# A linear-attention recurrence fused with a squared-ReLU layer: r in a four-token layout, a smaller copy of w, v cast on GpSimd's queue, and a searched order

## Chip, cores and metric

The kernel runs on one core of one Trainium2 chip. Its metric is the device time of an execution in microseconds; lower is better. Engines: PE is TensorE, ACT ScalarE, DVE VectorE, POOL GpSimd, and SP SyncE, which here only issues DMAs.

## The reference

Four batches, eight heads, 768 tokens, 48 features a head (`B, H, S, D = 4, 8, 768, 48`). An attention with a decaying state goes first:

```python
for t in range(S):
    cur = einsum('bhd,bhe->bhde', u * k[t], v[t])
    y[t] = einsum('bhd,bhde->bhe', r[t], state + cur)
    state = w[:, None] * state + einsum('bhd,bhe->bhde', k[t], v[t])
```

Then the heads are joined to `x` of 3072 x 384, and the layer is `relu(x @ w_in)**2 @ w_out` with `w_in` 384 x 2048 and `w_out` 2048 x 384. Inputs and outputs are float32.

## The kernel before

**Tiling.** The tokens go in chunks of 128. A unit is one chunk of one batch, so there are 24, in the order chunk by chunk (`units`, four batches a chunk). Within a chunk the recurrence is done by matmuls: r is multiplied by a power of w that grows with the token's place in its chunk, k by one that falls (`scale`, line 321, into the bf16 tile `rkw`). Heads go in pairs, padded from 48 to 64 features.

**One unit.** r, k and v are loaded by SP (`load`, line 300), each 128 tokens x 8 heads x 48 in rows of 192 bytes. `scale` is two DVE instructions. `rkw` is then turned so that features lie on partitions (`rkT`): for units 0 to 5 (`NPE = 6`) by PE (`turn`, line 341) and an ACT eviction (line 345), for the others by a DMA transpose on SP's queue (`turn_dma`, line 330). `at` (line 358) makes the 128 x 128 products of k and r, `mask` (line 370) keeps their upper triangle, `sums` (lines 378 and 383) makes the diagonal term with u and the unit's contribution to the state, `diag_v` (line 392), `state_add`, `state_decay` and `state_cast` (lines 400 to 412) carry on the state, `y_mm` (lines 421 and 427) and `evict_y` (line 436) make y. v is cast to bf16 by ACT (`cast_v`, line 325). y is turned by PE and ACT for units 0 to 5 (lines 452 and 456), otherwise by a DMA transpose (line 445).

**The layer.** `mm1` (line 468) makes blocks of 128 x 512 of the hidden layer, each followed by a ReLU on ACT (line 476) and a square on ACT or DVE (lines 483 and 485; `SQUARES = 'AMAMAAAM'` gives the engine of each in turn, A for ACT). `mm2` (line 492) multiplies by `w_out`, ACT evicts (line 499), SP stores (line 528). Some units go through `mm1` in pairs (`GROUPS`). The last unit is done in two column parts (`mm2_half`, line 508).

**Weights.** `w_in` and `w_out` are loaded in four quarters each, as a casting DMA by POOL (`weights`, lines 306 to 312). Before each, POOL copies one column of an r, k or v tile into `gate`, so the transfer is not issued before that tile has landed. `FRONT` lists the quarters with their gate tiles: w_in's first is gated on k of unit 1, all others on k of unit 3.

**Order.** The order on every engine is written by the class `Plan`, not found at run time. Each step has an engine, a cost in us, what it needs, what buffers and PSUM banks it takes, and a rank; for a DMA, `move` has the costs of its transfer. `Plan.run` plays the engines forward in time and always gives a free engine the ready step of lowest rank. Up to a planned time of 16 us, PE gets fill matmuls on a constant tile (`fill`, line 276) where it has nothing ready. Each engine then runs its list in order and waits on semaphores.

**Powers of w.** `wrow` is w as one row of 384, copied to all 128 partitions (line 222); `lnw` is its logarithm (line 241); `wpos` and `wneg` are exponentials with a scale for each partition (line 245). `rkw_b` are `NPAD = 5` padded buffers whose padding DVE clears (line 252).

Of the kernel before, what the change touches and what calls it, by code (L numbers as in the profile page):

```python
# [16 lines left out]
class Plan:  # L17
# [9 lines left out]
    def __init__(self, lags, cold, spare):  # L27
        self.lags = lags
        self.cold = cold
        self.spare = spare  # L30
        self.steps = []
        self.at = {}
        self.users = {}
        self.place = {}

    def add(self, key, engine, cost, emit, needs=(), rank=0.0, new=(), uses=(), move=None):
        s = dict(key=key, engine=engine, cost=cost, emit=emit, rank=rank, new=new, move=move)
        s["needs"] = [n for n in needs if n is not None]
        self.at[key] = s
        self.steps.append(s)  # L40
        for x in tuple(new) + tuple(uses):
            self.users.setdefault(x, []).append(s)

    def run(self, room, banks, count):
# [10 lines left out]
        begin, until, tight, loose = self.spare  # L55
        held[0] = "spare"
# [7 lines left out]
        def ready(s, e):  # L64
            if s["move"]:
                return s["end"] + moved
# [36 lines left out]
        while left:  # L103
            if held[0] == "spare" and t > until:
                held[0] = None
            for e, mine in todo.items():
# [5 lines left out]
                for s in mine:  # L112
                    if s["move"] and sum(x[1] / x[0]["move"][0] * x[0]["move"][3] for x in queues[e]) > 1.5:
                        continue
                    if all(done(self.at[k], e) for k in s["needs"]) and fits(s):
                        mine.remove(s)
                        left -= 1
                        for x in s["new"]:
                            if x[0] in banks:
                                n = min((n for n in held if held[n] is None), key=lambda n: since[n])  # L120
# [42 lines left out]
def kernel(  # L163
# [33 lines left out]
    loads = ctx.enter_context(tc.tile_pool(name="loads", bufs=6))  # L197
# [5 lines left out]
    banks = [psum.tile([128, 512], F32, name=f"bank{n}") for n in range(8)]  # L203
    plan = Plan((0.9, 0.0, 0.2, 0.33, 0.12), (5.5, 1.9), (1.25, 16.0, 0.057, 0.08))

    def bank(*key):
        return banks[plan.place[key]]
# [17 lines left out]
    nc.vector.memset(warm, 1.0)  # L225
    wu = const.tile([HP, 2, 2, 64], F32)
# [3 lines left out]
    nc.gpsimd.dma_start(out=wu[:, 1, :, :D], in_=u.rearrange("(p o) d -> p o d", o=2))  # L230

    iota_i = const.tile([128, 1], mybir.dt.int32)
    nc.gpsimd.iota(iota_i, pattern=[[0, 1]], base=0, channel_multiplier=1)
# [4 lines left out]
    ident4 = const.tile([HP, HP], F32)  # L238
    make_identity(nc, ident4)
    lnw = const.tile([128, dm], F32)  # L240
    nc.scalar.activation(lnw, wrow, AF.Ln)
    wpos = const.tile([128, H, D], F32)
    wneg = const.tile([128, H, D], F32)
    for wx, by in ((wpos, up), (wneg, down)):
        nc.scalar.activation(wx.rearrange("p h d -> p (h d)"), lnw, AF.Exp, scale=by)
# [15 lines left out]
    st32 = [const.tile([128, HP, D], F32, name=f"st32_{b}") for b in range(B)]  # L261
    stb = [const.tile([128, HP, 2 * D], BF16, name=f"stb_{b}") for b in range(B)]
    for b in range(B):
        nc.vector.memset(stb[b], 0.0)

    wend_c = const.tile([128, HP], F32)
    wend = wend_c.unsqueeze(2).to_broadcast([128, HP, D])
# [27 lines left out]

    def load(i, name):
        c, b = units[i]
        src = {"rt": r, "kt": k, "vt": v}[name]
        x = loads.tile([C, H, D], F32, name=name)
        nc.sync.dma_start(  # L300
            out=x, in_=src[b, :, c * C : (c + 1) * C, :].rearrange("h s d -> s h d")
        )
# [14 lines left out]
    def scale(i, x):  # L317
        t = tiles[i]
        t["rkw"] = rkw_b[i % NPAD]
        src, wx = (t["kt"], wneg) if x else (t["rt"], wpos)  # L320
        nc.vector.tensor_tensor(t["rkw"][:, x, :, :, :D], pair(src), pair(wx), ALU.mult)  # L321

    def cast_v(i):
        tiles[i]["vb"] = work.tile([C, H, D], BF16, name="vb")
        nc.scalar.copy(tiles[i]["vb"], tiles[i]["vt"])  # L325

    def turn_dma(i):
        t = tiles[i]
        t["rkT"] = work.tile([128, 2, HP, C], BF16, name="rkT")
# [5 lines left out]
    def turn(i, x):  # L335
        t = tiles[i]
        t["tp", x] = bank("h", i, "rk", x).bitcast(BF16)[:, : HP * C].rearrange("p (a c) -> p a c", a=HP)
        if x == 0:
            t["rkT"] = work.tile([128, 2, HP, C], BF16, name="rkT")
        for p in range(HP):  # L340
            nc.tensor.transpose(t["tp", x][:, p, :], t["rkw"][:, x, p].rearrange("p o e -> p (o e)"), identb)  # L341
# [198 lines left out]

    add("w", ACT, 3.9, None, rank=-1e3)
    add("wk", ACT, 0.48, None, rank=-1e3, needs=["w"])
    copy("begin", SP, 0.74, None, rank=-1e3)
    add("wu", POOL, 4.6, None, rank=-1e3)
# [3 lines left out]
    add("wend", ACT, 0.4, end_columns, rank=10, needs=["copied"])  # L548
# [165 lines left out]
```

## Time and profile before

| | us |
|---|---|
| median of 3 runs | 178.38 (178.34 to 178.59) |
| the profiled execution | 179.7 |
| its span | 177.9 |
| PE busy, of it fill matmuls | 167.5, 11.9 |
| DVE busy | 128.7 |
| ACT busy | 128.8 |
| POOL busy | 11.4 |

The span is the time from the first to the last instruction of the profiled execution; the execution's own time has what lies around it as well. Busy time of an engine leaves out instructions that issue DMAs or handle semaphores. PE counts as busy in fill matmuls, so a high share there does not mean useful work. The granted clock of TensorE is full in all 40 slices of the span.

### The profile page before, as it was taken

Reading aid. Unit: us, or ns where it says so; the run is one execution under the profiler, and the core shown is the slowest. Engines: PE = TensorE matmul, PEld = TensorE weight load, DVE = VectorE, ACT = ScalarE, POOL = GpSimd, SP = SyncE. Lnnn points to the kernel's source line nnn. Section 1 sums busy time; section 2 is a strip of 40 time slices with the busy share of each in tenths; the row PEclk is TensorE's granted clock in tenths of the full one; section 3 lists DMA queues with packets and bytes.
Section 4 is the critical chain, followed back from the end, with each engine's and each line's share of the span. In section 5 each row is a group of like instructions: output and inputs, shape, how many; then the busy total and the mean of one; then the engine's idle time right before and its main releaser. Section 6 shows DMA issues by size and latency. Waiting matters only on the chain.

```text
span 177.9 us, 5106 instructions
## 1 busy us (share of the span) xinstructions
PE 167.5 (94%) x2080; PEld 135.2 (76%) x2080; DVE 128.7 (72%) x279; ACT 128.8 (72%) x268; POOL 11.4 (6%) x35
## 2 busy tenths in 40 slices
PE   7699689999999999989979999899999999999993
PEld 7599479977786886876776796786795797878762
DVE  3389996565989899769779698589598695853100
ACT  2738889999385985597488599488597499659820
POOL 7120950000000000000000000000000000000000
PEclk9999999999999999999999999999999999999999
DMA  5999999999797888869879889999998897940212
GB/s 103 192 179 181 163 197 197 208 190 179 93 208 128 169 155 171 175 132 206 174 161 185 176 166 191 133 201 185 163 199 172 187 201 135 314 135 0 71 67 90
DMA packets 107385, 29.05 MB, mean 163 GB/s; under 512 B 101985, under 2 KB 106849, under 8 KB 107361
## 3 DMA queue, kind: packets, MB, share of 16 engines
q1 hardware_dynamic: 104976, 25.37, 75.1%
q0 software_dynamic: 2240, 3.15, 10.0%
q8 instruction: 16, 0.26, 0.6%
q10 hardware_dynamic: 144, 0.20, 0.6%
q14 instruction: 9, 0.07, 0.1%
HBM read 20.65 MB, written 4.72 MB: 143 GB/s over the span
## 4 chain that ended last, share of the span: by engine, by line
PE 57%; DMA 18%; DVE 17%; issue 3%; ACT 2%; SPq 1%; ACTq 0%
PE bank L492 22%; PE bank L468 22%; DMA rkT<-rkw 8%; DMA rt<-in_r_dram 5%; DVE am L370 4%; DVE rkw L321 4%; DVE yb L436 3%; PE bank L358 3%; DMA xT<-yb 2%; PE bank L276 2%; DMA wrow<-in_w_dram 2%; DVE dv L392 2%; DVE g L485 2%; PE bank L421 1%; PE bank L508 1%
## 5 line engine op out<-in xcount | busy, mean ns | idle before, releaser
L468 PE MATMUL bank<-xT,w_in_q 128*128 128x128 bf16 (+1 forms) x864 | 71.8, 237 | 0.5 <-ACT xT L456 0.3
L476 ACT ACTIVATE gr<-bank 128x512 f32<-128x512 f32 x96 | 55.0, 601 | 19.5 <-PE bank L468 18.9
L468 PEld LDWEIGHTS <-w_in_q 128*128 128x128 bf16 x864 | 64.4, 114 | 3.3 <-issue 0.7
L492 PE MATMUL bank<-w_out_q,g 128*128 128x384 bf16 x368 | 65.1, 326 | 0.0
L492 PEld LDWEIGHTS <-g 128*128 128x128 bf16 x368 | 34.4, 98 | 20.0
L370 DVE TENSOR_TENSOR am<-bank,smask 128x512 bf16<-128x512 f32 x48 | 31.8, 684 | 8.2 <-PE bank L358 8.1
L483 ACT ACTIVATE g<-gr 128x512 bf16<-128x512 f32 x60 | 37.3, 639 | 0.6
L485 DVE TENSOR_TENSOR g<-gr 128x512 bf16<-128x512 f32 x36 | 24.6, 687 | 13.1 <-ACT gr L476 13.0
L499 ACT COPY osb<-bank 128x384 f32<-128x384 f32 x23 | 11.0, 484 | 10.1 <-PE bank L492 7.9
L412 ACT CAST stb<-st 64x192 bf16<-64x192 f32 x40 | 14.0, 350 | 5.1 <-DVE st L406 4.4
L350 DVE TENSOR_TENSOR rk<-rkT 128x512 bf16<-128x512 bf16 x24 | 10.1, 422 | 7.7 <-DMA rkT<-rkw 5.6
L321 DVE TENSOR_TENSOR rkw<-rt,wpos 128x384 bf16<-128x384 f32 x24 | 13.2, 552 | 2.5 <-DMA rt<-in_r_dram 1.7
L436 DVE TENSOR_TENSOR yb<-bank,dv 128x384 bf16<-128x384 f32 x24 | 13.3, 555 | 2.3 <-PE bank L427 1.7
L392 DVE TENSOR_TENSOR dv<-vb,bank 128x384 f32<-128x384 bf16 x24 | 13.1, 545 | 2.6 <-PE bank L383 2.6
L321 DVE TENSOR_TENSOR rkw<-kt,wneg 128x384 bf16<-128x384 f32 x24 | 13.2, 551 | 0.6 <-DMA kt<-in_k_dram 0.3
L276 PE MATMUL bank<-warm 128*128 128x128 bf16 x108 | 11.9, 275 | 1.1 <-DVE warm L225 1.1
L358 PE MATMUL bank<-rkT 64*128 64x128 bf16 x192 | 9.8, 222 | 2.8 <-DMA rkT<-rkw 1.9
L325 ACT CAST vb<-vt 128x384 bf16<-128x384 f32 x24 | 12.2, 508 | 0.2
L402 DVE TENSOR_TENSOR st<-bank,st 64x192 f32<-64x192 f32 x32 | 11.3, 352 | 0.2
L358 PEld LDWEIGHTS <-rkT 64*128 64x128 bf16 x192 | 5.5, 96 | 7.5 <-issue 2.9
L276 PEld LDWEIGHTS <-warm 128*128 128x128 bf16 x108 | 9.6, 128 | 1.4 <-DVE warm L225 1.1
L345 ACT COPY rkT<-bank 128x512 bf16<-128x512 bf16 x12 | 6.9, 585 | 4.5 <-PE bank L341 4.5
(54 smaller groups left out, 97.8 us busy)
## 6 DMA issues: line engine op xcount, KB each, us to landing
rt<-in_r_dram SPq DMA_DIRECT2D x24, 192.0 KB, 4.2
kt<-in_k_dram SPq DMA_DIRECT2D x24, 192.0 KB, 4.0
vt<-in_v_dram SPq DMA_DIRECT2D x24, 192.0 KB, 4.4
out_dram<-osb SPq DMA_DIRECT2D x23, 192.0 KB, 2.8
w_in_q<-in_moe_w_in_dram POOLq DMA_DIRECT2D x4, 384.0 KB, 7.2
w_out_q<-in_moe_w_out_dram POOLq DMA_DIRECT2D x4, 384.0 KB, 13.1
rkT<-rkw SPq DMA_TRANSPOSE x18, 3.8
xT<-yb SPq DMA_TRANSPOSE x18, 3.0
```

The costliest lines, as they stand in the source:

```text
L276: nc.tensor.matmul(out=banks[0][:, :128], lhsT=warm, rhs=warm, start=True, stop=True)
L321: nc.vector.tensor_tensor(t["rkw"][:, x, :, :, :D], pair(src), pair(wx), ALU.mult)
L358: nc.tensor.matmul(out=t["at"][o][:, p, :], lhsT=t["rkT"][sl, 1, p, :], rhs=t["rkT"][sl, 0, p, :], start=True, stop=True,)
L370: nc.vector.tensor_tensor(am, t["at"][o], smask.unsqueeze(1).to_broadcast([C, HP, C]), ALU.mult)
L392: nc.vector.tensor_tensor(t["dv"], t["vb"], t["d"].unsqueeze(2).to_broadcast([C, H, D]), ALU.mult)
L412: nc.scalar.copy(stb[b][sl, :, o * D : (o + 1) * D], st32[b][sl])
L436: nc.vector.tensor_tensor(t["yb"], t["y"], t["dv"].rearrange("p h d -> p (h d)"), ALU.add)
L468: nc.tensor.matmul(out=t["h", s][:, a], lhsT=turned, rhs=chunks[c]["xT"][:, n, b : b + m, :], start=(n == 0), stop=(n == NK - 1),)
L476: nc.scalar.activation(t["gr", s], t["h", s], AF.Relu)
L483: nc.scalar.activation(g, x, AF.Square)
L485: nc.vector.tensor_tensor(g, x, x, ALU.mult)
L492: nc.tensor.matmul(out=t["o"], lhsT=chunks[units[i][0]]["g"][:, f, units[i][1], :], rhs=w_out_q[f // 4][:, f % 4, :], start=(f == 0), stop ...
```

## The change

1. **r of units 0 to 5** is loaded as four tokens a partition: two transfers, one for the even and one for the odd heads, in rows of 768 bytes. Partition p holds tokens 4(p // 4) to 4(p // 4) + 3 of head pair p % 4. `scale` multiplies by `wfour`, and `turn` becomes a matmul with the identity whose f32 output is written with a stride of four columns, which puts the tokens in order.
2. **w** is copied as 96 elements a partition (a head pair, by p % 4). `wfour` comes from it by four exponentials. Four f32 matmuls spread the logarithm to all pairs in PSUM, from where `wneg` and `wpos` are made. Four of the PSUM banks are used for that first and taken over later.
3. **v of units 6 to 23** is loaded by POOL's casting DMA straight to bf16 (`load_v`), into eight buffers; ACT's cast and SP's load of them go.
4. **State**: the float32 state is kept at 128 x 4 x 96 (with zero off-diagonal blocks) instead of 128 x 4 x 48, so an addition and a cast are one instruction instead of two, and a decay covers twice the columns.
5. **Order**: ranks of many steps come from a table `TURNS`; some costs of the planner, the gates in `FRONT`, the numbers of buffers and `SQUARES` are others; six of the padded buffers are cleared by POOL.

```diff
-    def __init__(self, lags, cold, spare):
+    def __init__(self, lags, cold, spare, turns):
+        self.turns = turns
...
     def add(self, key, engine, cost, emit, needs=(), rank=0.0, new=(), uses=(), move=None):
+        kind, which = (key[0], key[1] if len(key) == 2 else key[1:]) if isinstance(key, tuple) else ("", key)
+        rank = self.turns.get(kind, {}).get(which, rank)
...
-    NPAD = 5
-    SQUARES = 'AMAMAAAM'
+    NPAD = 8
+    NVB = 8
+    LATE = (0.0, 0.0, 0.0)
+    SQUARES = 'AAAMAAAM'
+    TURNS = {
...
+        "rt": {
+            0: -64.166, 1: -42.375, 12: 25.855, 16: 42.933, 17: 48.579, 18: 50.891, 2: -34.64, 20: 66.748, 22:
+            72.798, 3: -23.999, 5: -7.239, 7: 5.797, 8: 7.925
+        },
+        "kt": {
+            0: -62.034, 1: -59.051, 11: 22.767, 12: 25.913, 14: 31.199, 16: 41.23, 19: 60.057, 2: -36.564, 20:
+            63.314, 22: 67.009, 23: 62.992, 3: -23.719, 4: -15.851, 6: 5.385, 7: 6.643, 9: 9.761
+        },
+        "vt": {
+            0: -53.396, 1: -30.556, 2: -24.635
+        },
...
     FRONT = (
-        ("I", 0, ("kt", 1)), ("I", 1, ("kt", 3)), ("I", 2, ("kt", 3)), ("O", 0, ("kt", 3)),
-        ("I", 3, ("kt", 3)), ("O", 1, ("kt", 3)), ("O", 2, ("kt", 3)), ("O", 3, ("kt", 3)),
+        ("I", 0, ("rt", 1)), ("I", 1, ("rt", 2)), ("I", 2, ("rt", 3)), ("O", 0, ("kt", 3)),
+        ("O", 1, ("kt", 4)), ("O", 2, ("rt", 5)), ("O", 3, ("rt", 5)), ("I", 3, ("kt", 3)),
     )
...
-    loads = ctx.enter_context(tc.tile_pool(name="loads", bufs=6))
+    loads = ctx.enter_context(tc.tile_pool(name="loads", bufs=7))
...
-    wrow = const.tile([128, dm], F32)
-    nc.scalar.dma_start(out=wrow, in_=w.rearrange("h d -> (h d)").unsqueeze(0).to_broadcast([128, dm]))
+    wrow = const.tile([128, 2 * D], F32)
+    nc.scalar.dma_start(out=wrow, in_=w.rearrange("(a o) d -> a (o d)", o=2).unsqueeze(0).to_broadcast([32, HP, 2 * D]))
...
-    for n in range(NPAD):
-        for x in range(2):
-            nc.vector.memset(rkw_b[n][:, x, :, :, D:], 0.0)
+    for n in range(2):
+        nc.vector.memset(rkw_b[n][:, :, :, :, D:].rearrange("p x a o e -> p (x a o) e"), 0.0)
...
+    for n in range(2, NPAD):
+        nc.gpsimd.memset(rkw_b[n][:, :, :, :, D:].rearrange("p x a o e -> p (x a o) e"), 0.0)
...
+    def spread_log():
+        for a in range(HP):
+            sl = slice(a * 32, a * 32 + 32)
+            nc.tensor.matmul(out=four[:, a, : 2 * D], lhsT=ones[sl], rhs=lnw[sl], start=True, stop=True)
+
+    def power_four():
+        for l in range(4):
+            nc.scalar.activation(wfour[:, l].rearrange("p o d -> p (o d)"), lnw, AF.Exp, scale=at4[:, l : l + 1])
+
+    def power(out, by):
+        nc.scalar.activation(out.rearrange("p (a o) d -> p a (o d)", o=2), four[:, :, : 2 * D], AF.Exp, scale=by)
...
+        if name == "rt" and i < NPE:
+            src = src.rearrange("(a o) (q l) d -> o q a (l d)", o=2, l=4)
+            for o in range(2):
+                nc.sync.dma_start(out=x[:, o * 4 : o * 4 + 4, :].rearrange("p l d -> p (l d)"), in_=src[o])
+        else:
+            nc.sync.dma_start(out=x, in_=src.rearrange("h s d -> s h d"))
...
+    def load_v(i):
+        c, b = units[i]
+        tiles[i]["vb"] = work.tile([C, H, D], BF16, name="vc", bufs=NVB)
+        nc.gpsimd.dma_start(out=tiles[i]["vb"], in_=v[b, :, c * C : (c + 1) * C, :].rearrange("h s d -> s h d"))
...
+            if x == 0:
+                to = t["tp", 0].rearrange("p a (q l) -> p l q a", l=4)[:, p]
+                nc.tensor.matmul(out=to, lhsT=src, rhs=identb, start=True, stop=True)
...
-        for o in range(2):
-            sl = slice(o * 64, o * 64 + 64)
-            x = tiles[i]["s"][sl, :, o * D : (o + 1) * D]
-            if c == 0:
-                nc.vector.tensor_tensor(st32[b][sl], x, wend[sl], ALU.mult)
-            else:
-                nc.vector.tensor_tensor(st32[b][sl], x, st32[b][sl], ALU.add)
+        nc.vector.tensor_tensor(st32[b], tiles[i]["s"], st32[b] if c else wend, ALU.add if c else ALU.mult)
...
-        for o in range(2):
-            sl = slice(o * 64, o * 64 + 64)
-            nc.scalar.copy(stb[b][sl, :, o * D : (o + 1) * D], st32[b][sl])
+        nc.scalar.copy(stb[b], st32[b])
...
+            copy(("vb", i), POOL, 1.1, do(load_v, i), rank=a + 50, needs=[("kt", i - 1)], move=(1.06, 16, 1.4, 0.0, LATE[0]), new=[("vc", i)])
...
-        rt=6, kt=6, vt=6, rkw=NPAD, g=2, rkT=4, vb=4, rk=4, am=8, dv=4, yb=4, xT=3, gr=6, osb=6,
+        rt=7, kt=7, vt=7, rkw=NPAD, g=2, rkT=6, vb=6, vc=NVB, rk=4, am=8, dv=4, yb=4, xT=3, gr=6, osb=6,
```

More of the change, by code (lines that the diff above doesn't have):

```diff
@@ L225 @@
     nc.vector.memset(warm, 1.0)
+    I32 = mybir.dt.int32
+    iota_i = const.tile([128, 1], I32)
+    nc.gpsimd.iota(iota_i, pattern=[[0, 1]], base=0, channel_multiplier=1)
     wu = const.tile([HP, 2, 2, 64], F32)
@@ L328, in turn_dma @@
         t = tiles[i]
-        t["rkT"] = work.tile([128, 2, HP, C], BF16, name="rkT")
+        t["rkT"] = work.tile([128, 2, HP, C], BF16, name="rkT", bufs=6)
         nc.sync.dma_start_transpose(
@@ L539 @@
     plan.fill = fill
[L541 to L544, printed above, removed]
+    add("w0", ACT, 3.2, None, rank=-1e3)
+    add("log", PE, 0.25, spread_log, rank=-1e3, needs=["w0"], new=[("log", n) for n in range(4)])
+    add("w", ACT, 1.0, power_four, rank=-1e3, needs=["w0"])
+    add("wk", ACT, 0.48, do(power, wneg, down), rank=-999, needs=["log", "w"], uses=[("log", n) for n in range(4)])
+    add("wr", ACT, 0.48, do(power, wpos, up), rank=-998, needs=["wk"], uses=[("log", n) for n in range(4)])
+    add("wu", POOL, 5.8, None, rank=-1e3)
     add("cols", PE, 0.1, spread_columns, rank=-50, needs=["wu"], new=[("h", "cols")])
@@ L547 @@
     add("uwb", POOL, 0.75, u_columns, rank=-200, needs=["copied"])
-    add("wend", ACT, 0.4, end_columns, rank=10, needs=["copied"])
+    add("end", ACT, 0.4, end_columns, rank=0, needs=["copied"])
+    add("wend", POOL, 0.8, end_blocks, rank=1.5, needs=["end"])
     for n, (what, q, gated) in enumerate(FRONT):
@@ L551 @@
             (what, q), POOL, 1.0, do(weights, gated, q, what), rank=n,
-            move=((2.35, 98, 1.25, 0.0) if what == "I" else (2.05, 78, 1.25, 0.0)), needs=[gated], uses=[gated],
+            move=((2.35, 98, 1.9, 0.0, 0.0) if what == "I" else (2.05, 78, 1.9, 0.0, 0.0)), needs=[gated], uses=[gated],
         )
@@ L586 @@
         else:
-            copy(("rkT", i), SP, 1.24, do(turn_dma, i), rank=a - 30, needs=both, move=(1.5, 26, 0.67, 1.0), new=[("rkT", i)], uses=[("rkw", i)])
+            copy(("rkT", i), SP, 1.24, do(turn_dma, i), rank=a - 30, needs=both, move=(1.5, 26, 0.67, 1.0, LATE[1]), new=[("rkT", i)], uses=[("rkw", i)])
         add(("rk", i), DVE, 0.335, do(rk, i), rank=a + 1, needs=[("rkT", i)], new=[("rk", i)], uses=[("rkT", i)])
@@ L632 @@
         else:
-            copy(("xT", i), SP, 1.2, do(x_dma, i), rank=a - 30, needs=xneed, move=(0.6, 26, 0.67, 0.4), new=xnew, uses=[("yb", i)] + xuse)
+            copy(("xT", i), SP, 1.2, do(x_dma, i), rank=a - 30, needs=xneed, move=(0.6, 26, 0.67, 0.4, LATE[2]), new=xnew, uses=[("yb", i)] + xuse)
     begun = 0
```

176 lines of the change are left out of this document (135 added, 41 removed), and 13 rows, old and new, of the table TURNS.

## The prediction

> **What bounds the kernel now.** I read the page's head first, then a table of busy time by stage, then the fill matmuls, TensorE's idle gaps, the weight transfers, and last the rates of the DMA engines.
>
> ```profile
> PE 167.5 (94%) x2080; PEld 135.2 (76%) x2080; DVE 128.7 (72%) x279; ACT 128.8 (72%) x268; POOL 11.4 (6%) x35
> ...
> DMA  5999999999797888869879889999998897940212
> ```
>
> TensorE (PE) is the bound by its share, but the share hides two things: it counts the fill matmuls of line 276, and it averages over stages. The DMA engines are full or nearly so from 4 us to 150 us. The table by stage (length; busy us of PE, PEld, DVE, ACT, POOL; clock, DMA share, GB/s):
>
> ```profile
> 0.00:16.00 16.00, 13.48 (x166) 12.37 (x167) 9.56 (x34) 8.36 (x17) 4.74 (x21) 1.00 1.02 167
> 16.00:26.70 10.70, 8.58 (x156) 7.13 (x154) 10.51 (x24) 9.21 (x20) 6.63 (x14) 1.00 1.03 173
> 26.70:60.00 33.30, 33.30 (x480) 27.12 (x478) 25.29 (x52) 27.15 (x58) 0.00 (x0) 1.00 0.99 172
> 60.00:140.00 80.00, 77.13 (x856) 60.36 (x854) 66.28 (x140) 58.72 (x126) 0.00 (x0) 1.00 0.92 172
> 140.00:175.10 35.10, 35.00 (x435) 28.23 (x433) 16.82 (x32) 25.33 (x50) 0.00 (x0) 1.00 0.55 137
> ```
>
> From 26.7 to 175.1 PE stands idle for 2.97 us in all. So time can come only from two places: what PE does not use before 26.7, and those 2.97 us. The tail after PE's last matmul is 2.8 us and is not touched. The same table for the fill alone gives 10.79 us before 16.0 and 1.14 us from 16.0 to 26.7. Useful PE work before 26.7 is therefore 2.69 + 7.44 = 10.1 us, and 16.6 us are lost there.
>
> The gaps of PE after 60 us (start, length, ..., in brackets the idle time before and its releaser):
>
> ```profile
> 80.15 0.27 PE L421 MATMUL bank<-vb,am 128*128 128x48 bf16 x4 [0.55 <-DVE am L370]
> ...
> 89.86 0.40 PE L358 MATMUL bank<-rkT 64*128 64x128 bf16 x8 [1.02 <-DMA rkT<-rkw]
> ...
> 116.08 0.40 PE L358 MATMUL bank<-rkT 64*128 64x128 bf16 x8 [0.93 <-DMA rkT<-rkw]
> ...
> 139.29 2.13 PE L468 MATMUL bank<-xT,w_in_q 128*128 128x256 bf16 x18 [0.25 <-DMA xT<-yb]
> ```
>
> They add to 2.75 us, and 2.20 of it waits for DMA transposes. These sit on SP's queue between the loads.
>
> What holds PE back before 26.7 is the weights. GpSimd issues a quarter of w_in only when its gate tile has been read, and the second gate waits long:
>
> ```profile
> 18.04 0.46 POOL L306 COPY gate<-kt 128x1 f32<-128x1 f32 x1 [7.08 <-DMA kt<-in_k_dram]
> 18.51 0.78 POOL L309 DMA_DIRECT2D w_in_q<-in_moe_w_in_dram  x1
> ```
>
> By issue plus landing, w_in's first quarter is there at 10.17 + 6.3 = 16.5, the second at 18.51 + 6.2 = 24.7, and the rest of all weights follow 2.1 to 2.8 us apart until 38.9. PE's first block of the first layer starts at 16.84, and it is saturated once the second quarter is in.
>
> The early loads of 192 KB land 1.0 to 1.1 us apart (r, k, v of unit 0 at 5.34, 6.4, 7.5, then 8.45, 9.5, 10.6): 192-byte rows at some 185 GB/s. What longer rows do is seen in 150 to 156 us, where six stores with 1536-byte rows run almost alone from the middle on:
>
> ```profile
> GB/s 9 10 3 0 8 90 128 141 209 253 256 230 215 264 217 227 258 270 253 249 203 236 358 420 358 430 369 400 369 403 379 358 399 348 348 410 338 410 369 430
> ```
>
> So 350 to 430 GB/s for 1536-byte rows, about double.
>
> **The change, part by part.** All durations are of the profiled execution: 177.9 us of span, 179.7 us in all. The runs' median is 178.38, that is span + 0.5, and I convert so.
>
> *First loads.* The copy of w shrinks from 192 to 48 KB. It now lands at 4.37, together with r of unit 0 (5.34). It saves 144 KB, which is 0.4 us at the store's rate and 0.8 at the loads'. r of a unit becomes two transfers with 768-byte rows: between 0.5 us (store rate) and 1.03 (no gain) instead of 1.03; I take 0.65, nearer to the store, as only row length differs. k of unit 0, third in the queue, then lands 0.4 to 1.2 us earlier; I take 1.1, less some 0.3 because r takes a second issue on SP (0.45 each). Six loads of r save 6 x 0.38 = 2.3 us of full DMA engines by 40 us.
>
> *Powers of w.* Before: logarithm 0.52, two exponentials 0.61 and 0.60, done at 6.07. After: a logarithm and four exponentials over 128x96. The nearest rows are 0.20 for 128x4 and 0.5 to 0.6 for 128x384, hence about 0.3 each, 1.5 together, then the two of 384 columns read from PSUM (0.6 each, as gr). That is 1.0 us more of ScalarE (ACT), but it begins earlier and r's factor needs only the first 1.5: at about 3.4 + 1.5 = 4.9 instead of 5.56. k's factor needs 0.6 more, 5.5, against k's arrival at 6.4 now. Four f32 matmuls (0.26 each in the nearest row, L281's) stand where PE runs fill. So unit 0 starts about 0.8 us earlier.
>
> *Weights' order.* The first quarter is gated on r of unit 1 instead of k of unit 1. By the new ranks the loads go r0, k0, k1, v0, r1; 2 x 0.65 + 3 x 1.03 = 4.4 us of transfer against 5.1 for the five to k1 now, with 0.5 us of w's copy less in front: about 1.2 us sooner, landing at 15.3. The larger step is the second quarter, gated on r2 (two loads later, about 3 us beside the first quarter) instead of k3: issued at about 12 instead of 18.5, landing 2.5 us or more behind the first, at 18 to 19 instead of 24.7. The third follows at 21.
>
> *What that gives PE.* From 16.0 to 26.7 PE loses 3.26 us now; with two quarters and two or three units ready, I expect 2.5 of it filled (bounds 1 and 3.2). Before 16.0, 13.3 us are lost; unit 0 is 0.8 us earlier, the attention matmuls of unit 0 now wait behind fourteen fill matmuls (8.00 to 9.70, while their operand's eviction ended at 8.83), and the one addition of a state (0.55, as yb, instead of 2 x 0.352) brings VectorE's pace from 4.17 us a unit (yb at 13.40, 17.57, 21.75) to 4.0. I take 1.3 (0.5 to 2.5). Together 3.8. ACT caps this: 3.8 us of PE are 5.7 blocks of 0.67, each a relu (0.60) and three quarters of a square (0.64 x 0.75), 1.08 in all, so 6.2 us of ACT. ACT has 4.5 us idle from 4.4 to 16.0, 1.5 to 26.7, then none (13.09 busy of 13.3 to 40.0). Less 1.0 for the powers, plus 4 x 0.2 for the state's cast, that is 5.8, not all usable. I take 3.3 for the front (1.5 to 5.3).
>
> *The strided turn of r.* 24 matmuls write f32 columns 16 bytes apart. No row here does so. Four now take 0.22 us, 0.055 each; the bounds are no loss, and L281's 0.264 each. Twelve of them (units 0 to 2) stand beside fill, twelve on the path: 0 to 2.5 us. I take 0.4, near the first bound, as they have the same columns and type as L341. The eviction, f32 instead of bf16, goes from 0.585 to 0.60.
>
> The Trainium skill's page "PSUM — Partial Sum Buffer", section Specifications (TRN2), says PSUM has 8-byte lines and that a non-contiguous pattern slows matmuls significantly. One word a line instead of two would double these matmuls; as an estimate, the twelve on the path would add 12 x 0.055 = 0.7 us, and the sum below would be 0.3 us longer.
>
> *Units 6 to 23.* ACT loses 18 casts x 0.508 = 9.1 us and 20 x (0.70 - 0.51) = 3.8 in state casts, and gains 12 squares x 0.639 = 7.7 (60 to 72 of 96). VectorE loses 12 x 0.687 = 8.2 of squares and 20 x 0.15 = 3.0 of state additions, and gains 16 x 0.2 = 3.2 in decays over 384 columns. Both run beside PE; cover is their 28% of idle time, and the 0.55 us gap behind a mask should close. SP loses 18 issues of 0.53 to 1.7 us standing in front of transposes; GpSimd gets 18 with 1024 rows each. Its rows are 0.53 to 0.58 for 128 rows and 0.75 to 0.80 for 384, so 1.3 by the line through them, 24 us in all on an engine idle since 24.7. Casting halves the bytes written, not the rows or the bytes read. Of 2.75 us I expect 1.7 back (-1 to 2.5).
>
> *Memsets.* Six pads move to GpSimd (0.2 to 0.3 each by its rows), covered by its wait from 4.4 to 7.5; uncovered they would delay u's columns by at most 1.5 us, for unit 0 only.
>
> Sum: 3.3 + 1.7 - 0.4 = 4.6. Span 173.3, median **173.8**.
>
> **The rivals.**
> *DMA stays the bound in the middle.* 0.92 of share from 60 to 140, and the two waits on transposes are waits for transfers; v still moves, only from another queue, and with eight buffers it can run ahead of what is urgent. Then the middle gives nothing: 178.4 - 3.3 + 0.4 = 175.5. Against it: transposes stood behind v's issues. The Trainium skill's page "DMA: Bandwidth & Descriptors", section Issuing engines are not separate DMA queues, has this rule: another issuing engine saves only issue time.
> *The front gives its bound.* ACT finds the room, the middle closes: 178.4 - 5.3 - 2.3 + 0.3 = 171.1.
> *Slower: casting rows load the DMA engines more.* No cast transfer is in this trace. GpSimd's queue spent 10.0% x 16 x 177.9 / 2240 = 127 ns a packet, SP's 20 ns, though for rows some six times as long. Slack is 0.08 x 80 = 6.4 us, plus 2.3 and 0.5 saved. If a cast v takes x us more than 1.03, 18x - 9.2 is lost; slower than before from x = 0.77. At x = 1.03 (double) it is 9.3 - 4.6 = 4.7 slower: 183.1. Against it: 384 KB of weights landed every 2.1 to 2.8 us beside loads.
> *Long rows of r gain nothing* (256 columns of q and a, two issues): only order is left, about 1 us: 177.4.
>
> **How the numbers follow.** Forecast 0.55, DMA-bound middle 0.17, front's bound 0.14, slower 0.11, no gain of rows 0.03. About 0.2% (0.35 us) is what a measurement can tell from no change. Faster 0.87, same 0.02, slower 0.11. The range leaves out the slower case and the far end of the front's: 170.8 to 177.6.
>
> **What would show it.** Right: second quarter of w_in landed by 19, L468 blocks dense from 18, PE saturated by some 23; idle after that under 1.5 us; no v on SP after unit 5. Wrong: L341 for r at over 0.1 us apiece; v landing late with PE or VectorE waiting for it; rkT waits over 1 us between 60 and 140; gr on ACT late before 40.

## The result, and the profile after

| | before | after |
|---|---|---|
| median of the runs, us | 178.36 (177.07 to 178.59) | 185.53 (184.99 to 187.03) |
| profiled execution, its span | 179.7, 177.9 | 185.25, 183.3 |
| PE busy, of it fill | 167.5, 11.9 | 168.8, 9.6 |
| PE idle (span less busy) | 10.4 | 14.5 |
| DVE, ACT, POOL busy | 128.7, 128.8, 11.4 | 119.2, 123.3, 30.1 |

The kernel became slower: 1.043 times the time before (95% interval 1.035 to 1.051). The forecast was 173.8. Single executions of some of the kernels below lie 6 us and more apart; a ratio leaves out those over 1.5% above the fastest of their kernel, a median counts them all. All ratios here are to runs of the kernel before on the same chip. Four chips were used (one each for e1 to e4, e5 to e8, e9 to e12 and e13 to e18), so between these groups the ratios are the safer comparison.

The head of the page of the kernel after, and its table by stage (length; busy us of PE, PEld, DVE, ACT, POOL; clock, DMA share, GB/s):

```profile
PE 168.8 (92%) x2079; PEld 135.9 (74%) x2079; DVE 119.2 (65%) x244; ACT 123.3 (67%) x246; POOL 30.1 (16%) x62
...
DMA  4999999999999999999999999989999710041022
```

```profile
0.00:16.00 16.00, 13.78 (x191) 12.49 (x191) 11.33 (x34) 9.41 (x21) 10.35 (x34) 1.00 0.87 164
16.00:26.70 10.70, 8.50 (x147) 7.99 (x147) 4.57 (x10) 8.94 (x19) 2.67 (x6) 1.00 1.16 202
26.70:60.00 33.30, 31.23 (x406) 24.06 (x407) 23.10 (x47) 23.48 (x47) 9.26 (x13) 0.95 1.39 165
60.00:140.00 80.00, 75.95 (x868) 60.41 (x866) 65.92 (x131) 55.61 (x110) 7.87 (x9) 1.00 1.23 171
140.00:180.00 40.00, 39.21 (x472) 30.91 (x469) 13.95 (x25) 25.86 (x50) 0.00 (x0) 1.00 0.29 74
```

Three things stand in it. Before 26.7 us the change does what was forecast: PE is busy for 22.28 us, of which 9.56 are fill, so 12.7 us are useful against 10.1. From 26.7 to 60, where PE had not stood idle at all, it now loses 2.07 us and some of its clock. From 60 to 140 it loses 4.05 us where it lost 2.87. The time that packets took has gone up (share 1.39 and 1.23 against 0.99 and 0.92) while the bytes have not (165 and 171 GB/s against 172 and 172).

The gaps of PE (start, length, ..., in brackets the idle time before and its releaser):

```profile
26.88 0.61 PE L488 MATMUL bank<-identb,rkw 128*128 128x128 bf16 x4 [1.03 <-DVE rkw L459]
...
31.49 0.48 PE L532 MATMUL bank<-vb,rkw 128*128 128x96 bf16 x4 [1.56 <-ACT vb L468]
...
62.95 2.87 PE L609 MATMUL bank<-xT,w_in_q 128*128 128x128 bf16 x48 [0.90 <-DMA xT<-yb]
...
72.74 2.84 PE L609 MATMUL bank<-xT,w_in_q 128*128 128x128 bf16 x48 [1.20 <-DMA xT<-yb]
...
118.24 2.02 PE L609 MATMUL bank<-xT,w_in_q 128*128 128x256 bf16 x17 [0.56 <-DMA xT<-yb]
```

The waits on `rkT` have fallen from 1.9 to 0.8 us. In their place PE stands at the head of whole blocks of the layer (L609) and waits for `xT`, the turned y. Behind the gap of 1.56 us the clock falls; the same columns in stretches of 1 us:

```profile
31.00:32.00 1.00, 0.51 (x5) 0.42 (x5) 0.28 (x1) 1.00 (x3) 0.40 (x2) 0.54 1.01 191
32.00:33.00 1.00, 1.00 (x4) 0.44 (x3) 0.93 (x2) 1.00 (x3) 1.00 (x4) 0.50 1.08 196
33.00:34.00 1.00, 1.00 (x11) 0.96 (x9) 0.97 (x3) 0.89 (x3) 1.00 (x2) 0.50 1.04 126
34.00:35.00 1.00, 1.00 (x16) 1.00 (x15) 0.15 (x1) 0.83 (x3) 1.00 (x2) 0.76 0.99 172
```

That is 0.46 + 0.50 + 0.50 + 0.24 = 1.7 us of clock. The span is 5.4 us longer: 4.1 more idle, 2.3 less fill, and 3.6 more busy time for the same work, 1.7 of it by the clock and 1.4 by the strided turn (below). But the clock cannot be the main loss: another execution of this kernel took 185.8 us at full clock.

### The profile page after: what moved, and what is told of

Same layout as the page of the kernel before. It is cut to its first block, busy times and chain, and to the rows that moved or that the text cites. A ratio compares the mean times of both kernels' runs of the same rounds, so it can differ in the third digit from the quotient of the medians.

```text
span 183.3 us, 5067 instructions
## 1 busy us (share of the span) xinstructions
PE 168.8 (92%) x2079; PEld 135.9 (74%) x2079; DVE 119.2 (65%) x244; ACT 123.3 (67%) x246; POOL 30.1 (16%) x62
## 5 line engine op out<-in xcount | busy, mean ns | idle before, releaser
L609 PE MATMUL bank<-xT,w_in_q 128*128 128x128 bf16 (+1 forms) x864 | 71.0, 238 | 4.3 <-DMA xT<-yb 2.7
L609 PEld LDWEIGHTS <-w_in_q 128*128 128x128 bf16 x864 | 65.5, 114 | 7.3 <-issue 2.5
L633 PE MATMUL bank<-w_out_q,g 128*128 128x384 bf16 x368 | 68.0, 328 | 0.6 <-ACT g L624 0.6
L624 ACT ACTIVATE g<-gr 128x512 bf16<-128x512 f32 x72 | 44.4, 640 | 0.6
L626 DVE TENSOR_TENSOR g<-gr 128x512 bf16<-128x512 f32 x24 | 16.4, 686 | 20.2 <-ACT gr L617 20.2
L464 POOL DMA_DIRECT2D vc<-in_v_dram x18 | 15.8, 892 | 64.3 <-PE bank L568 52.1
L553 ACT CAST stb<-st 128x384 bf16<-128x384 f32 x20 | 10.4, 524 | 8.4 <-DVE st L549 8.4
L456 DVE TENSOR_TENSOR rkw<-rt,wpos 128x384 bf16<-128x384 f32 x18 | 9.7, 549 | 4.6 <-DMA rt<-in_r_dram 4.6
L541 DVE TENSOR_TENSOR dv<-vc,bank 128x384 f32<-128x384 bf16 x18 | 9.8, 545 | 3.6 <-ACT g L624 3.6
L390 PE MATMUL bank<-warm 128*128 128x128 bf16 x99 | 9.6, 255 | 1.1 <-DVE warm L328 1.1
L562 PEld LDWEIGHTS <-am 128*128 128x128 bf16 x192 | 7.8, 96 | 2.7 <-DVE am L519 1.5
L549 DVE TENSOR_TENSOR st<-st,wend 128x384 f32<-128x384 f32 x16 | 8.8, 550 | 0.0
```

The lines of the kernel that those rows point to most:

```text
L464: nc.gpsimd.dma_start(out=tiles[i]["vb"], in_=v[b, :, c * C : (c + 1) * C, :].rearrange("h s d -> s h d"))
L609: nc.tensor.matmul(out=t["h", s][:, a], lhsT=turned, rhs=chunks[c]["xT"][:, n, b : b + m, :], start=(n == 0), stop=(n == NK - 1),)
L624: nc.scalar.activation(g, x, AF.Square)
L626: nc.vector.tensor_tensor(g, x, x, ALU.mult)
L633: nc.tensor.matmul(out=t["o"], lhsT=chunks[units[i][0]]["g"][:, f, units[i][1], :], rhs=w_out_q[f // 4][:, f % 4, :], start=(f == 0), stop ...
```

## The experiments

Four suspects were set against each other: the order table `TURNS`, the weights' gates in `FRONT`, r's layout, and v on GpSimd's queue.

### Taking the table and the queue out of the change

e1 empties the table, so every step has its written rank; e2 leaves the table and puts v of units 6 to 23 back on SP with ACT's cast; e3 does both; e4 is e1 with r loaded and turned as before.

```diff
-    TURNS = { ... }                                            # e1, e3, e4
+    TURNS = {}
-        for n, name in enumerate(("rt", "kt", "vt") if i < NPE else ("rt", "kt")):   # e2, e3; ACT's cast for all units
+        for n, name in enumerate(("rt", "kt", "vt")):
...
-        if name == "rt" and i < NPE:                           # e4; scaling and turn as before, too
+        if name == "rt" and i < 0:
...
```

> The changed kernel with an empty table TURNS: every step has its default rank again, all else as changed. Order theory (the searched ranks are the loss: they let y of some units, its transposes and so the next blocks come late, and hold loads of units 3 and 4 behind weights): back by 8 to 11 us, 174 to 178, TensorE idle after 35 us under 2 us instead of 5.2. Queue theory (GpSimd's casting loads of v, eight of which go out from 33 to 40 us, slow SP's loads and transposes): the loss stays, 183 to 186.

> The changed kernel with v of units 6 to 23 loaded by SP and cast by ScalarE again, the table TURNS kept. Order theory: no help, 184 to 187, as the order of y and of the blocks is unchanged. Queue theory: the share of DMA between 35 and 60 us falls from over 1.3 to about 1, the waits for xT at 63 and 73 us go, 177 to 180.

> Default ranks and v on SP and ScalarE. Order theory: v's queue is a small item, within 1.5 us of the run with default ranks alone, in either direction. Queue theory: about 177 to 179, well below the run with default ranks alone. If both matter, below both of the others.

> Default ranks, and r of units 0 to 5 loaded in 192-byte rows and turned by plain transposes again. If the long rows are worth what was forecast (2.3 us of DMA time by 40 us, unit 0 earlier), 1 to 3 us slower than the run with default ranks alone. If the strided turn (0.10 us a matmul instead of 0.055, 24 of them) eats it, within 0.5 us.

| | median us | ratio to before |
|---|---|---|
| e1 default ranks | 180.58 | 1.011 (1.000 to 1.023) |
| e2 v on SP | 185.43 | 1.043 (1.035 to 1.052) |
| e3 both | 180.40 | 1.012 (1.001 to 1.022) |
| e4 e1, r as before | 179.53 | 1.011 (1.003 to 1.018) |

The table costs 5 us of the 7.2. Neither with the table (e2 against the change) nor without it (e3 against e1) does v's queue make a difference, and r's layout makes none in this setting either (e4 against e1). The table by stage of e2 says the same of the packets' time: with v on SP its share falls to 0.90 and 0.97, about what it was before the change, and the time of the kernel stays.

```profile
26.70:60.00 33.30, 31.59 (x415) 24.34 (x410) 23.64 (x47) 24.55 (x51) 1.36 (x4) 0.95 0.90 160
60.00:140.00 80.00, 75.22 (x861) 59.30 (x859) 60.52 (x120) 60.39 (x121) 0.00 (x0) 1.00 0.97 181
```

Of e1, the largest gap of PE behind 16 us and the window from 60 to 140:

```profile
23.35 0.69 PE L398 MATMUL bank<-identb,rkw 128*128 128x128 bf16 x4 [2.07 <-DVE rkw L369]
```

```profile
60.00:140.00 80.00, 80.00 (x921) 63.71 (x922) 67.05 (x132) 59.72 (x118) 7.00 (x8) 1.00 1.16 174
```

Without the table the middle is full, with v still on GpSimd's queue. What PE loses in this trace, it loses before 30 us: behind the gap of 2.07 us its clock is 0.50 from 24 to 27. But this is e1's fastest execution (178.05 us, no more than before); where those of 180.6 us lose the rest is not shown.

### The table and the gates by themselves, on the kernel before

e6 is the kernel before with only `TURNS` added (and the line in `Plan.add` that reads it); e7 is it with only the new `FRONT`; e5 is e1 with the old `FRONT`; e8 is e1 with fill until a planned 24 us instead of 16 and 30 fill matmuls ahead of the turn of r of unit 4.

```diff
+    TURNS = { ... }                                            # e6, as in the change
...
-        ("I", 0, ("kt", 1)), ("I", 1, ("kt", 3)), ("I", 2, ("kt", 3)), ("O", 0, ("kt", 3)),   # e7; e5 the reverse
+        ("I", 0, ("rt", 1)), ("I", 1, ("rt", 2)), ("I", 2, ("rt", 3)), ("O", 0, ("kt", 3)),
...
+        for _ in range(30 if i == 4 and x == 0 else 0):        # e8, in turn()
+            fill()
...
```

> Default ranks and the weights' gates as before the change (first quarter on k of unit 1, all others on k of unit 3); v, r, w, state and squares as changed. Gate theory (of the loss left with default ranks, the earlier weights take the DMA engines from the loads of units 3 and 4; TensorE idles 2 us near 22 and its granted clock then falls to half for some 3 us): r of unit 4 is scaled in time, no wait over 1 us before 30, clock 1.0 throughout, 1 to 4 us below the run with default ranks alone, 175 to 179. Rival (the rest is lost elsewhere, as by the wider state or the strided turn): no better than the run with default ranks.

> The kernel before, with the table TURNS of the change and nothing else of it. Order theory: slower by 5 to 8 us, 182 to 186, with TensorE waiting between 60 and 140 us for xT and rkT. Rival (the ranks suit the changed kernel's costs and hurt only through its gates): within 2 us of before.

> The kernel before, with the weights' gates of the change and nothing else of it. Gate theory: the loads of units 3 to 5 come later, TensorE idles and its clock falls near 22 to 30, 1 to 4 us slower, 179 to 182. What was forecast (the earlier second quarter fills TensorE): 2 to 3 us faster, 175 to 176.

> Default ranks, with fill matmuls up to a planned time of 24 us and thirty more in front of the turn of r of unit 4, where TensorE stood idle for 2.07 us; nothing else. If the lowered clock after that gap costs: the clock stays at 1.0 from 23 to 28 us and the time falls by 1 to 2 us against default ranks alone, with less scatter. If the late loads alone cost: within 0.7 us.

| | median us | ratio to before |
|---|---|---|
| e5 e1, old gates | 182.81 | 1.017 (1.007 to 1.028) |
| e6 before, table | 188.47 | 1.060 (1.052 to 1.067) |
| e7 before, new gates | 181.64 | 1.023 (1.013 to 1.034) |
| e8 e1, more fill | 181.22 | 1.012 (1.002 to 1.023) |

The table alone, with r's layout, casts, gates and state as before, costs over 10 us. From e6's table by stage and its gaps:

```profile
0.00:16.00 16.00, 11.35 (x164) 10.14 (x164) 8.91 (x32) 7.06 (x15) 5.15 (x21) 1.00 0.96 165
16.00:26.70 10.70, 7.51 (x117) 6.44 (x112) 8.58 (x18) 7.52 (x17) 6.13 (x14) 0.80 1.13 195
...
60.00:140.00 80.00, 75.02 (x865) 59.51 (x863) 65.53 (x140) 59.55 (x124) 0.00 (x0) 0.98 0.95 178
```

```profile
74.74 0.27 PE L515 MATMUL bank<-vb,am 128*128 128x48 bf16 x4 [1.99 <-DVE am L464]
...
77.41 6.88 PE L562 MATMUL bank<-xT,w_in_q 128*128 128x128 bf16 x72 [1.36 <-DMA xT<-yb]
```

Idle PE time up to 26.7 is 7.84 us against 4.64, and from 60 to 140 it is 4.98 against 2.87. Again PE waits at the head of a long block of the layer (72 matmuls) for y that comes late. The gaps are not the whole price: the clock is 0.80 from 16 to 26.7, 0.96 from there to 60 and 0.98 from 60 to 140 where it is 1.00 before, some 5 us of clock by the lengths of these stages.

The new gates alone (e7) do not gain the front's 2 to 3 us but lose 2.3%. In e5 the old gates were expected to help and did not; between e1 and e5 the intervals overlap. Fill held e8's clock at 1.00 through the front without a gain over e1, so nothing shows that e1 is behind by its half clock. (The profiled execution of e8 is one of 183.2 us, with its largest wait, 2.91 us for `rkT`, at 58.38; the fastest took 179.38.)

### Which entries of the table

e9 keeps only the 13 entries of `at` and `y` out of the 198 of the change's table; e16 is e6 without these.

```diff
+    TURNS = {k: TURNS[k] for k in ("at", "y")}                                    # e9
+    TURNS = {k: x for k, x in TURNS.items() if k not in ("at", "y")}              # e16
```

> The changed kernel with TURNS cut to its entries for at and y (13 of some 170); all other steps have default ranks. If the harm of the table lies in its entries for the recurrence (y of units 7, 11, 15 and 22 and at of units 15, 21 and 22 pushed behind later blocks, so that their state and their turned y come late): slower than default ranks by 4 us or more, 184 to 189, with TensorE waiting for xT or masks. If it is spread over the table or sits in the loads: within 2 us of default ranks, 179 to 182.

> The kernel before with the table TURNS, but without its entries for at and y. If those 13 entries are the harm of the table: 178 to 181, against 188 with the whole table. If the rest of the table (loads, blocks of the first layer, masks) is as bad: 184 or more.

e9 took 193.25 us, 1.083 (1.075 to 1.091), slower than with the whole table; e16 took 186.05, 1.041 (1.033 to 1.049). e9's longest wait is of the same kind:

```profile
74.48 5.78 PE L610 MATMUL bank<-xT,w_in_q 128*128 128x128 bf16 x60 [2.86 <-DMA xT<-yb]
```

So the harm is not in one entry: either part, and they have no entry in common, makes its kernel slower than it is with an empty table. The 13 ranks of `at` and `y` cost more without the entries around them, and the others cost some 7.6 us without them (186.05 against 178.40 for the runs of before beside it).

### What of the rest costs, and what gains

With the written ranks the parts can be seen singly. e10 is e5 with v on SP; e11 is e10 with r as before. What e11 still has of the change is the small copy of w with its spread logarithm, the wide state, the other `SQUARES`, the memsets, the numbers of buffers and the planner's costs. e12 is the kernel before with the wide state alone (and the planner's costs of its steps).

```diff
-        for n, name in enumerate(("rt", "kt", "vt") if i < NPE else ("rt", "kt")):   # e10, e11
+        for n, name in enumerate(("rt", "kt", "vt")):
...
-            swift = n == 0 and i < NPE                         # e11: planned cost of r's load 1.06, not 0.65
+            swift = False
...
-        for o in range(2):                                     # e12: state_add; state_cast likewise
...
+        nc.vector.tensor_tensor(st32[b], tiles[i]["s"], st32[b] if c else wend, ALU.add if c else ALU.mult)
...
```

> Default ranks, gates as before, v of units 6 to 23 on SP and ScalarE. Queue theory in its small form (v's eight early transfers from 31 to 39 us delay k of unit 5 and the transposes of unit 6, where the run with default ranks and gates of before waited 1.80 and 1.92 us): those two waits shrink below 1 us together, 177 to 180 against 180 to 184. If v's queue does not matter: 180 to 184 again.

> As the last, and r of units 0 to 5 in 192-byte rows, turned by plain transposes. What is left of the change is the copy of w, the wider state, the squares, the memsets on GpSimd, the buffers and the planner's costs. If the long rows gain: slower than the last by 1 us or more. If the second issue of r on SP (0.6 us each in the changed profile) and the strided turn eat the gain: equal to it within 1 us, 177 to 180.

> The kernel before with the state at 128 x 4 x 96 and nothing else: one addition and one cast a unit instead of two, a decay of 384 columns. As forecast VectorE's pace in the front falls from 4.17 to 4.0 us a unit; TensorE's start gains 0.5 us at most. 177 to 179, within 0.5% of before. If the wider state is what is left of the loss: 180 or more.

| | median us | ratio to before |
|---|---|---|
| e10 | 181.56 (177.57 to 183.91) | 1.004 (0.999 to 1.009) |
| e11 | 177.28 (176.72 to 177.97) | 0.995 (0.993 to 0.998) |
| e12 | 178.78 (178.00 to 179.93) | 1.006 (1.002 to 1.010) |

e11 is the only version whose ratio lies clearly below 1, by 0.5% (0.2 to 0.7). The wide state alone is 0.6% slower, so the gain is in the other parts, which were not taken apart. r's layout costs 0.9% by the ratios (1.6 us), or 4.3 us by the medians of all ten executions of each; the ratio leaves out six of e10's ten. The profiled execution of e10 is one of these six (183.6 us). It differs from e11's at k of unit 5, in e10 first and then in e11:

```profile
39.23 0.61 PE L400 MATMUL bank<-identb,rkw 128*128 128x128 bf16 x4 [2.98 <-DVE rkw L366]
```

```profile
39.30 0.39 PE L396 MATMUL bank<-identb,rkw 128*128 128x128 bf16 x4
```

The turn starts at the same time in both. In e10 PE waited 2.98 us for it; in e11 PE did 20 matmuls of the layer just ahead of it. k of unit 5 lands at 38.6 in e10 (issued 21.32, 17.3 to land) and at 37.6 in e11 (18.18 + 19.4): the long rows of r bring the later loads no sooner. But the planner prices such a load at 0.65 us instead of 1.06, takes k for landed earlier, and writes the turn six steps further ahead in PE's list. The list is the same in every execution of e10; whether PE waits as long in those of 177.6 to 179.8 us is not shown. Three further runs were to split that cost:

```diff
-                nc.sync.dma_start(out=x[:, o * 4 : o * 4 + 4, :]..., in_=src[o])                 # e14, from e10
+                (nc.sync, nc.scalar)[o].dma_start(out=x[:, o * 4 : o * 4 + 4, :]..., in_=src[o])
...
-            nc.tensor.transpose(t["tp", x][:, p, :], src, identb)                                # e15, from e11, x == 0
+                to = t["tp", 0].rearrange("p a (q l) -> p l q a", l=4)[:, p]
+                nc.tensor.matmul(out=to, lhsT=src, rhs=identb, start=True, stop=True)
...
-            nc.sync.dma_start(out=x, in_=src.rearrange("h s d -> s h d"))                        # e18, from e11, r of units 0 to 5
+            for o in range(2):
+                nc.sync.dma_start(out=x[:, o * 4 : o * 4 + 4], in_=src[o * 4 : o * 4 + 4].rearrange("h s d -> s h d"))
```

> Default ranks, gates as before, v on SP, r in long rows, but its second transfer issued by ScalarE instead of SP. If SP's second issue of r (six of some 0.65 us, which pushes k of unit 5 behind the burst of weights, where it landed at 38.5 us) is what the long rows cost: k of unit 5 is issued about 3 us earlier, the wait of 2.98 us before 39 us goes, 176 to 178.5. If the strided turn is what costs: still 179 to 183.

> The run of 177.3 us (default ranks, gates, v and r's loads as before) with one thing changed: the turn of r of units 0 to 5 writes f32 columns 16 bytes apart, as in the change. The tokens of r of these units come out permuted, so y of these units is that of another order; the work is the same. If the strided write costs what its matmuls show (0.10 us instead of 0.055, six times four of them, half on the path): 177.4 to 178.5. If it is most of the long rows' cost: 179 or more.

> The run of 177.3 us (ranks, gates, v and r as before the change) with r of units 0 to 5 loaded in two transfers of 96 KB each, four heads a transfer, still in 192-byte rows. If SP's second issue is what long rows cost (six times some 0.6 us; k of unit 5 issued after the burst of weights): 179 to 182, with TensorE waiting near 38 us for k of unit 5. If not: 177 to 178.5.

e14 took 190.18 us, 1.062 (1.052 to 1.071), by a wait of its own, so it says nothing on r's second issue on SP (the trace is of an execution of 195.94 us):

```profile
36.71 0.61 PE L417 MATMUL bank<-rkT 64*128 64x128 bf16 x8 [13.90 <-ACT rkT L404]
```

ACT starts nothing between 20.9 and 35.0 us; its next entry is r's second half, and the evictions that PE waits for stand in its list behind that.

e15, whose kernel leaves the tokens of r of units 0 to 5 out of order, took 177.84 us (1.005; 1.000 to 1.009). That is 0.6 us over e11 by the medians, and 1.0% or 1.7 us by the ratios; the two ran on different chips. A matmul of its strided turns is 337 ns long on average against 238 of a plain one (they overlap); all 24 keep PE busy for 4.1 us against 2.6.

e18 took 176.51, 176.86, 179.55 and 180.44 us. The profiled execution has a span of 174.6, no wait near 38 us, and k of unit 5 at 37.4 (19.77 + 17.6). A second issue is not shown to cost anything, nor is a cost excluded.

### v's queue with nothing else in the way

e13 is e11 with v of units 6 to 23 on GpSimd's casting queue; e17 is e13 with three buffers for it instead of eight.

```diff
-        for n, name in enumerate(("rt", "kt", "vt")):          # e13
+        for n, name in enumerate(("rt", "kt", "vt") if i < NPE else ("rt", "kt")):
...
-    NVB = 8                                                    # e17, from e13
+    NVB = 3
```

> Default ranks, gates and r as before, v of units 6 to 23 by GpSimd's casting queue: the run of 177.3 us with v's queue put back. If v's queue is a gain once nothing else is in its way (ScalarE loses 9 us, SP 18 issues): 174 to 176.5. If its eight early transfers take the engines from the loads of units 5 to 7: 178 to 181. If it does not matter, 176.5 to 178.

> The run of 182.3 us (v on GpSimd's casting queue; ranks, gates and r as before the change) with three buffers for v instead of eight, so that only three transfers of v can go ahead before 35 us. If running ahead is the harm: SP's first transposes are issued in under 2 us each, TensorE's wait of 3.14 us before 54 us shrinks below 1 us, 176.5 to 179. If casting rows are dear wherever they run, or v now comes late: 181 to 184.

| | median us | ratio to before |
|---|---|---|
| e11 v on SP | 177.28 | 0.995 (0.993 to 0.998) |
| e13 GpSimd, eight buffers | 182.34 | 1.020 (1.014 to 1.027) |
| e17 GpSimd, three buffers | 178.86 | 1.000 (0.996 to 1.005) |

The queue costs 5 us here by the medians, 3.5 of them by running ahead (4.5 and 3.6 by the ratios; e11 ran on another chip). e13's timeline (SP's queue, PE, GpSimd) and its window from 40 to 60, then that of e17:

```profile
45.62 4.68 SPq L383 DMA_TRANSPOSE rkT<-rkw  x1
...
54.02 0.40 PE L413 MATMUL bank<-rkT 64*128 64x128 bf16 x8 [3.14 <-DMA rkT<-rkw]
...
59.02 0.87 POOL L374 DMA_DIRECT2D vc<-in_v_dram  x1 [20.36 <-PE bank L474]
```

```profile
40.00:60.00 20.00, 16.47 (x189) 11.50 (x187) 11.00 (x22) 9.64 (x20) 0.87 (x1) 0.91 1.50 151
```

```profile
40.00:60.00 20.00, 19.55 (x233) 13.74 (x230) 15.10 (x31) 10.95 (x22) 1.75 (x2) 1.00 1.11 140
```

GpSimd issues eight v from 24.4 to 38.7 us and then waits 20.36 us for a buffer, so v runs far ahead of its use. Meanwhile one transpose needs 4.68 us on SP's queue only to be issued (1.60 at the same place with three buffers), and PE waits 3.14 us for `rkT`. The packets' time tells the same: share 1.50 for 151 GB/s, 1.11 for 140 with three buffers, and 0.97 for 153 in e11 with v on SP. Running ahead alone is not enough, though: e1 issues eight v as early (31.1 to 38.7 us), its first two transposes take 1.38 and 2.24 us to issue, and PE has no such wait. In e11 the first took 2.57 us.

## Why the prediction was wrong, by its own steps

**The step that failed is one that is not in the sum: the order.** `TURNS` sets ranks for steps on every engine, and the prediction read from it only in which order the loads go. It priced the order at nothing, as if each wait of before would be shortened and none moved. With lists run in order that does not hold: a listed step whose input is late stops all behind it. e6 puts the price at over 10 us on the kernel before; in the change it is 5 (after against e1). Nor does the rest of the sum hold: without the table the kernel is still no faster than before (e1, 1.011; 1.000 to 1.023), so nothing is left of the 4.6 us. None of the rivals had the order as a loss. The slower rival (cast rows) had the sign and a near time, 183.1, for another reason.

**First loads and powers.** About right. k of unit 0 lands at 5.7 instead of 6.36, where 0.8 was forecast as the difference; r's first scale starts at 4.87 instead of 5.60. SP's second issue of r took 0.6 to 0.8 us, not 0.45.

**Weights.** Right in kind, late by about 1 us: the first quarter was issued at 10.51 and landed at 16.8 (forecast 15.3), the second at 11.64 and 19.6 (18 to 19), the third at 14.70 and 22.2 (21). GpSimd was late for the gates, since its two casts of u took 1.03 us instead of 0.44 and 1.14 us of `wend` came between:

```profile
8.09 1.03 POOL L416 CAST uwb<-cols 64x4 bf16<-64x4 f32 x2
9.18 1.14 POOL L425 COPY wend<-wend_c 64x192 f32<-64x192 f32 x2
10.39 0.18 POOL L440 COPY gate<-rt 128x1 f32<-128x1 f32 x1
10.51 0.80 POOL L443 DMA_DIRECT2D w_in_q<-in_moe_w_in_dram  x1
```

**The front's 3.3 us.** 2.6 came, and were given back. The prediction's account ended at 26.7 and took what follows for unchanged. But the DMA engines were full, as its own first view said, so weights that come earlier push loads back: k of units 3 and 4 landed at 19.3 and 22.6 instead of 17.9 and 21.1, and VectorE waited for k and r in turn:

```profile
22.63 0.56 DVE L456 TENSOR_TENSOR rkw<-kt,wneg 128x384 bf16<-128x384 f32 x1 [2.36 <-DMA kt<-in_k_dram]
...
26.26 0.56 DVE L459 TENSOR_TENSOR rkw<-rt,wfour 128x384 bf16<-128x384 f32 x1 [3.07 <-DMA rt<-in_r_dram]
```

The units then come late to PE between 26 and 35 us. In e7, where only the gates are new, the second quarter landed at 19.1 us, about as forecast, but k of units 3 and 4 landed at 19.7 and 30.3. PE's useful work before 26.7 us is 9.5 us there, less than the 10.1 of before, so the gates by themselves do not give the front's gain; they made the kernel before 2.3% slower. The change's waits from 26.7 to 60 come with the table: PE loses 0.1 us there in e7 and 0.6 in e1, whose gap of 2.07 us lies ahead of that, at 23.35.

**Long rows of r.** 0.38 us a load were booked as saved. k of unit 5 came no sooner for it (e10 against e11), and the layout as a whole costs about 0.9% there and nothing in e1 against e4. In e10's profiled execution the loss is a wait in front of a turn that the plan, counting on the gain, had put earlier; that is read from the two lists and was not tested alone. The rival "long rows gain nothing" was right that they gain nothing; that two issues are the reason is not shown (e18).

**The strided turn.** A group of four that starts from a stop takes 0.61 us (at 26.88 in the trace after) against 0.40 of a plain one (at 19.59 in the trace before), so each matmul takes 0.05 us more: some 0.10 against the 0.055 of the prediction. The forecast took 0.4 us for all, the run shows 0.6 (medians) to 1.7 (ratios; e15 against e11), so it may be as much as r's layout costs in all. The Trainium skill's page "PSUM — Partial Sum Buffer", Specifications (TRN2), says that a non-contiguous pattern slows matmuls significantly. The trace agrees, and the 0.7 us that had been estimated from it lies between those two values.

**Units 6 to 23.** The engines' savings were about right: ACT 5.5 us less in all (forecast 5.2 for these units), DVE 9.5 less (8.0). They are worth nothing, since neither was the bound: e11, the fastest, has ACT at 129.5. v's issue costs GpSimd 0.88 us, not 1.3. But no kernel is faster for having v on GpSimd's queue: in the middle e1's trace has no gap, where e3's, with v on SP, loses 1.92 us, yet both take 180.4 to 180.6 us, and with the old gates the queue is a loss (e13). So the "DMA-bound middle" held in its outcome, and in e13 more than it was put. By e13 and e17 what hurts there is v that runs ahead, which that rival named. The Trainium skill's page "DMA: Bandwidth & Descriptors", Issuing engines are not separate DMA queues, says that transfers started by different engines share the DMA engines and interleave; e13's 4.68 us issue and the wait of 3.14 us behind it agree. In the change as a whole this loss does not show (e2), and without the table neither (e3 against e1); why it needs the old gates stays open.

**Cast rows.** With three buffers the queue costs 1.6 us over e11, not the 4.7 and more of that rival, so the rows themselves are not shown to be dear; the packet times of e11, e17 and e13 rose with the number of transfers let ahead.

**What stays open:** which entries of the table do the harm; what in e11 gives the 0.5%; how r's cost divides between the strided turn, the plan's price and SP's second issue. The parts do not add up either: the gates alone cost 2.3% on the kernel before, yet e1 with the new gates is not slower than e5 with the old ones.

## What to carry to other kernels

Where every engine runs a fixed list, a change of order is a change of its own, and here it was the largest unknown: price it by trying it alone, and where that can't be done, widen the range. A planner whose cost for one load is 0.4 us too low can do harm beyond those 0.4 us (e10's wait of 2.98 us), since in-order engines then stop in front of work that is ready. On full DMA engines a transfer moved forward in time can take from those that are urgent (e7, e13), so limit how far it may run ahead, and follow the sum past the stage in which the gain appears.

## What the runs showed of the hardware

- PE's clock fell to 0.50 for 3.4 us (1.7 us lost at half speed) after gaps of 1.56 us (after) and 2.07 us (e1), but stayed full after 2.00 (e7) and 2.91 us (e8). The Trainium skill's page "TensorE: Matmul & The Clock Gate", Part 1, names an idle window of about 3.4 us; the traces have the drop after a single shorter gap (in the one after, with gaps of 1.03 and 0.33 us in the 5 us ahead of it), and differ there.
- The clock that the profile shows as full from 0 us on was not: fill matmuls mostly took 314 ns up to some 12 us in the trace before and up to 5.5 us in the one after, and 219 ns later (from 7.5 us in the one after). So busy times of the first 12 us of the two do not measure quite the same work.
- Matmuls that write f32 columns 16 bytes apart take some 0.10 us instead of 0.055 (after; one lasts 334 ns on average against 240 of a plain one).
- Issuing one DMA transpose on SP took 4.68 us where GpSimd's queue had run eight transfers ahead (e13), 1.60 at the same place with three (e17); but 1.38 in e1 with eight ahead, and 2.57 in e11 with none on that queue.
- Halving a transfer did not halve its issue: 0.6 to 0.8 us on SP for 96 KB of r, where 192 KB of k beside it took 0.59 (after) and the first ones before the change 0.45 to 1.0.
